# Three half-precision products in place of fp32 for kernel spectra and direct transforms in an S4 convolution and SwiGLU kernel

## The chip, the cores and the metric

The kernel runs on one core of a Trainium2 chip. The metric is device time in microseconds (us) of one execution; three executions before the change took 1172.26 to 1174.25 us, with a median of 1174.09 us. The engines are TensorE (PE, its weight loads PEld), VectorE (DVE), ScalarE (ACT), GpSimd (POOL) and SyncE (SP, which issues most DMAs). Each takes its instructions in the order of its own queue, and waits on semaphores for the others.

## The reference

Two layers, each an S4 convolution with a residual and a SwiGLU feed-forward network with a residual, on a sequence of L = 2048 rows with D = 512 channels; F = 1376, N = 128 states. Both layers use the same weights, so the convolution kernel K is formed once.

```python
def _A_ref(u, A_re, A_im, B_re, B_im, C_re, C_im, log_dt, Dskip):
    dt = jnp.exp(log_dt)[:, None]
    logdA = dt * (A_re + 1j * A_im)
    dB = dt * (B_re + 1j * B_im)
    P = jnp.exp(logdA[:, :, None] * l[None, None, :])
    K = jnp.einsum("dn,dnl,dn->dl", Cc, P, dB).real
    ...
    Yf = Uf * Kf[None, :, :, :]
    ...
    y = y + u * Dskip[None, None, :]

def _B_ref(x, w_gate, w_up, w_down):
    return (_silu(x @ w_gate) * (x @ w_up)) @ w_down

x = x + _A_ref(_layernorm(x), ...)
x = x + _B_ref(_layernorm(x), ...)
x = x + _A_ref(_layernorm(x), ...)
x = x + _B_ref(_layernorm(x), ...)
```

## The kernel before

**Stages.** The sequence is cut into four blocks of T = 512 rows. A block's transform is a product with constant factors of 128 by 128 (four residues q, real and imaginary part). Ahead of the blocks the kernel forms the convolution kernel's 2048 lags for 512 channels, in eight chunks of 64 channels, and transforms them. Then the eight pairs (layer, block) of SEQ follow, each an `ssm` (multiply by the spectra, inverse transform, residual) and an `ffn`.

**Order.** Everything up to the first `ffn` is traced inside `tc.manual_schedule` for ACT, DVE and PE: the order of each of these engines is the program's order, written by hand with generators, of which `take(it, n)` runs the next n steps. DMAs on SP are placed by a planner. A tile of a tag with n buffers waits until an earlier tile of that tag is done with. Tag "w" has three buffers of 2 KB per partition, "uu" three, and the PSUM tags "big" two and "sml" four.

**Start-up.** `stats` and `norm_early` normalise block 0 on DVE, `gen_w` forms the weights w0 (B, C and dt) on DVE, `gen_exp` and `gen_trig` run exponentials, sines and cosines on ACT. `direct` transforms block 0 straight from its rows with factors `ef` and `ek` (eight generators fw; the first step is the matmuls, L286, the second the eviction on ACT, L289). Block 1 is normalised (L964), written to `ndr`, and transformed by `second` one piece per pass and by two `early` pieces.

**The loop over chunks i = 0 to 6.** `lags` (L510, L511) forms chunk i's lags by small matmuls `pk`; ACT evicts them (`spread_in`, L516), PE rearranges them (`spread`, L526, L528, with the skip weights added by a matmul of one row), ACT evicts the result as `kt` (L1042), and `spectra` multiplies it with the factors (L547) for the four residues. ACT evicts each spectrum (L556, L558), and DVE (`wrap`, L584, L586) or POOL combines parts that go to `wdr`. Meanwhile DVE runs `gen_g` and `gen_e` for chunk i + 1 (L467 to L499 and L450 to L459) and `gen_turns` and `gen_reduce` for chunk i + 2 (L365 to L388). `gen_mags` (matmuls L438, exponentials L441) and `gen_trig` (L395 to L397) run for chunk i + 2. `norm_units` loads pieces of the FFN weights into tag "w", squares them on ACT (L316) and sums them on PE (L320). `sizes` sums the magnitudes of `kt` on ACT (L602); `product_scale` later makes from them a power of two, `sy`, by which products of blocks 1 and up are scaled ahead of half precision.

**The loop's order around `kt`.** `take(gg, 2)`, the last two steps of `gen_g`, ends with L499:

```python
            kp = spread(i, ks)
            if more:
                f = second(*sec[i])
                next(f)
            take(gg, 2)
            if more:
                tr = gen_trig(ts[i + 2])
                take(tr, 1)
            kt = kt2[:, 0]
            A.activation(kt, kp, AF.Copy)
            take(tr, 1)
```

**After the loop** the last chunk's lags and spectra are interleaved with `ssm(0, 0)`, whose inverse transform stays in fp32 (L781 with `ei`), and then the first `ffn` starts. From block 2 on, `forward` already uses three half-precision products, with the factors `eh` loaded then.

Of the kernel before, what the change touches and what calls it, by code (L numbers as in the profile page):

```python
# [41 lines left out]
HALF = 2  # L42
# [4 lines left out]
def dft_constants():  # L47
# [34 lines left out]
def kernel(ctx, tc, x, a_re, a_im, b_re, b_im, c_re, c_im, log_dt, d_skip,  # L82
                           w_gate, w_up, w_down, c_ef, c_ei, c_ek, c_am, c_eh, c_eih, out):
# [65 lines left out]
    hpi = sb.tile([P, 1], F32, name="hpi")  # L149
# [5 lines left out]
    ndr = dram.tile([2, 2, P, 2, HD], F32, name="ndr")  # L155
# [34 lines left out]
    nc.sync.dma_start(dsk, d_skip)  # L190

# [47 lines left out]
    def forward(n, h, eh):  # L239
# [13 lines left out]
        for i, q in enumerate(QORD):  # L253
            z = z2[:, 0 if eh else i % 2]
# [3 lines left out]
            if eh:  # L258
                hl = z2[:, 1].bitcast(F16).rearrange("p i (l d) -> p l i d", l=2)
                A.activation(hl[:, 0], z, AF.Copy, scale=256.0)  # L260
                stt(hl[:, 1], z, 256.0, hl[:, 0], OP.subtract)
            pf = psml([P, 2, HD], "pf")
            with tc.high_priority(offset=BOOST):
                for o in range(2):
                    if eh:
                        terms = [(eh[:, q, o + i, le], hl[:, lz, i]) for i in range(2) for le, lz in ((0, 0), (0, 1), (1, 0))]
                    else:
                        terms = [(ef[:, q, o + i], z[:, i]) for i in range(2)]
# [3 lines left out]
                A.activation(u, pf, AF.Copy, scale=2.0 ** -16 if eh else 1.0)  # L272
# [6 lines left out]

    def direct(b, h, q, n, space=psml):  # L280
# [8 lines left out]
        A.activation(u, pf, AF.Copy)  # L289
# [224 lines left out]
    def spread_in(pk):  # L514
        ks = tl([P, 4, 16, 16], "ks", "nn")
        A.activation(ks, pk.rearrange("p d (c a) -> p a c d", a=4), AF.Copy)  # L516
        return ks

    def spread(ch, ks):
# [3 lines left out]
        for grp in range(4):  # L523
            d0 = ch * DC + 16 * grp
            for ga in range(4):
                PE.matmul(kp[32 * ga:32 * ga + 32, grp], lhsT=ident[:, 32 * grp:32 * grp + 32], rhs=ks[:, ga],  # L526
                          start=True, stop=ga > 0, tile_position=(0, 32 * ga))
            PE.matmul(kp[0:32, grp, 0], lhsT=ident[0:1, 0:32], rhs=dsk[:, d0:d0 + 16], start=False, stop=True,  # L528
                      tile_position=(0, 0))
        return kp  # L530

    def spectra(ch, kt, k0, k1, qs=QORD, late=False):
# [4 lines left out]
        for q in qs:  # L537
# [6 lines left out]
            for i, c in [(i, c) for c in range(4) for i in range(2)] if k1 == 1 else \  # L544
                        [(i, c) for i in range(2) for c in range(4)]:
                e = ek[q // 2][:, q % 2, c - 1, i] if c else ef[:, q, i]
                PE.matmul(pw[:, i], lhsT=e, rhs=kt[:, :, c + 4 * k0:4 * k1:4, :].rearrange("p g k d -> p k g d"), start=c == 0, stop=c == 3)  # L547
                if k0 == 1 and (i, c) == (0, 3):
                    yield
# [140 lines left out]
    def inputs():  # L690

        for layer, b in SEQ:
# [17 lines left out]
            if (layer, b) == SEQ[HALF]:  # L710
                eh.append(tl([P, 4, 3, 2, P], "eh", "ef", F16))
# [213 lines left out]
    with tc.manual_schedule(engines={mybir.EngineType.Activation, mybir.EngineType.DVE, mybir.EngineType.PE}):  # L925
# [20 lines left out]
        for f in fw:  # L946
            next(f)
# [240 lines left out]
```

## Time and profile before

| | |
|---|---|
| median of three executions | 1174.09 us |
| span of the profiled execution | 1173.0 us |
| lag products of chunk 0 start | 58.7 us |
| lag products of chunk 7 end | 275.3 us |
| first FFN product starts | 320.5 us |

The profile comes from one execution. A line of a timeline has the start, the duration, the engine, the line of the program, the operation, out<-in with shapes, the count of merged instructions, and in brackets the idle time ahead of it with what ended it. In a line of groups the busy time and the mean duration stand behind the bar, then the idle time with its releaser. A matmul's duration contains its latency, so that neighbours overlap; their spacing is read from merged runs.

### The profile page before, as it was taken

The numbers are of one execution on the slowest core, as the hardware profiler recorded it, in microseconds if no ns is written. First come the engines' busy times: TensorE is split into PE (matmuls) and PEld (weight loads), VectorE is DVE, ScalarE is ACT, GpSimd is POOL, SyncE is SP. The second block draws the span as 40 slices with busy tenths as digits, with TensorE's granted clock in tenths as the row PEclk, the third lists the DMA queues.
The fourth block names the chain that finished last, engine by engine and source line by source line (L and its number), as shares of the span: only waits on it lengthen the run. The fifth ranks groups of instructions, "written<-read, shape, count | busy, mean of one in ns | idle before, by whom it ended". The sixth has DMA issues, their size and how long they took to land.

```text
span 1173.0 us, 25233 instructions
## 1 busy us (share of the span) xinstructions
PE 1103.5 (94%) x10276; PEld 861.6 (73%) x10276; DVE 1019.0 (87%) x1669; ACT 617.2 (53%) x1151; POOL 117.0 (10%) x170
## 2 busy tenths in 40 slices
PE   4899998989789989999999999999999999999998
PEld 3777777767675957686868687868777686876875
DVE  8999999997899999999998999999995999973211
ACT  6989898952382644537644533665434452333211
POOL 3110200013300010101000000211000000000000
PEclk9999999999999999999999999999999999999999
DMA  7454445576695237322253535342444144311000
GB/s 258 135 157 120 118 119 123 132 190 192 192 283 183 78 111 206 121 95 91 87 162 98 161 121 173 97 142 89 139 134 156 63 123 144 113 32 37 15 23 18
DMA packets 139174, 147.55 MB, mean 126 GB/s; under 512 B 78449, under 2 KB 87665, under 8 KB 139058
## 3 DMA queue, kind: packets, MB, share of 16 engines
q1 hardware_dynamic: 134194, 129.17, 36.4%
q0 software_dynamic: 4864, 16.78, 6.0%
q8 instruction: 80, 1.31, 0.5%
q14 instruction: 36, 0.29, 0.1%
HBM read 98.71 MB, written 28.31 MB: 108 GB/s over the span
## 4 chain that ended last, share of the span: by engine, by line
PE 40%; DVE 30%; ACT 13%; issue 9%; DMA 5%; POOL 2%; SPq 1%; DVEq 0%; ACTq 0%; POOLq 0%
PE pgu L886 6%; PE pgu L887 6%; PE pgu L888 6%; DVE yk L765 4%; DVE t L762 4%; PE pi L781 4%; PE pw L547 4%; PE py L900 3%; PE py L901 3%; PE py L902 3%; DVE z L226 2%; DVE yk L762 2%; PE pf L270 2%; DVE bt L226 2%; PE pk L510 2%
## 5 line engine op out<-in xcount | busy, mean ns | idle before, releaser
L886 PE MATMUL pgu<-mix,wsl 128*128 128x256 f16 x1280 | 350.5, 274 | 8.6 <-DVE sg L892 2.4
L887 PE MATMUL pgu<-mix,wsl 128*128 128x256 f16 x1280 | 350.6, 274 | 0.0
L888 PE MATMUL pgu<-mix,wsl 128*128 128x256 f16 x1280 | 350.5, 274 | 0.0
L887 PEld LDWEIGHTS <-wsl 128*128 128x128 f16 x1280 | 125.8, 98 | 24.7 <-issue 9.9
L888 PEld LDWEIGHTS <-wsl 128*128 128x128 f16 x1280 | 125.8, 98 | 15.1
L886 PEld LDWEIGHTS <-wsl 128*128 128x128 f16 x1280 | 125.8, 98 | 14.9
L900 PE MATMUL py<-wsl,hh 128*128 128x512 f16 (+1 forms) x352 | 133.6, 381 | 0.4 <-DVE sgr L862 0.4
L902 PE MATMUL py<-wsl,hl 128*128 128x512 f16 (+1 forms) x352 | 132.8, 381 | 0.0
L901 PE MATMUL py<-wsl,hh 128*128 128x512 f16 x320 | 121.5, 381 | 0.0
L762 DVE TENSOR_TENSOR t<-uu,w 128x1024 f32<-128x1024 f32 x96 | 117.5, 1224 | 0.5 <-DVE rs L222 0.3
L765 DVE TENSOR_TENSOR yk<-yk,t 128x1024 f32<-128x1024 f32 x96 | 117.5, 1224 | 0.2
L891 ACT ACTIVATE sg<-pgu,sc 128x512 f32<-128x512 f32 x80 | 54.6, 683 | 104.9 <-PE pgu L888 96.4
L892 DVE SCALAR_TENSOR_TENSOR sg<-pgu,sc,sg 128x512 f32<-128x512 f32 x80 | 60.0, 750 | 46.3 <-ACT sg L891 46.2
L781 PE MATMUL pi<-yl,mix 128*128 128x256 f16 x672 | 92.8, 273 | 6.4 <-ACT yl L770 5.5
L547 PE MATMUL pw<-kt,ek 128*128 128x256 f32 (+2 forms) x420 | 95.9, 365 | 0.0
L893 ACT ACTIVATE hh<-sg 128x512 f16<-128x512 f32 x80 | 50.0, 626 | 69.4 <-DVE sg L892 69.3
L547 PEld LDWEIGHTS pw<-kt,ek 128*128 128x128 f32 x420 | 76.3, 190 | 9.1
L270 PE MATMUL pf<-z,eh 128*128 128x256 f16 x576 | 75.0, 272 | 2.1 <-DVE z L226 1.7
L781 PEld LDWEIGHTS <-mix 128*128 128x128 f16 x672 | 65.3, 98 | 14.2 <-issue 1.1
L770 ACT ACTIVATE yl<-mix,sy 128x512 f16<-128x512 f32 x56 | 40.2, 718 | 59.1 <-DVE mix L767 58.8
L762 DVE TENSOR_TENSOR yk<-u,w0r 128x1024 f32<-128x1024 f32 x56 | 68.5, 1223 | 0.4 <-ACT u L272 0.4
L894 DVE TENSOR_TENSOR hl<-sg,hh 128x512 f16<-128x512 f32 x80 | 55.2, 691 | 13.5 <-ACT hh L893 13.5
(248 smaller groups left out, 2167.0 us busy)
## 6 DMA issues: line engine op xcount, KB each, us to landing
w<-wdr SPq DMA_DIRECT2D x96, 256.0 KB, 2.7
uu<-udr SPq DMA_DIRECT2D x96, 256.0 KB, 3.0
udr<-u POOLq DMA_DIRECT2D x32, 256.0 KB, 2.7
wdr<-wo SPq DMA_DIRECT2D x96, 64.0 KB, 2.6
udr<-u SPq DMA_DIRECT2D x16, 256.0 KB, 2.2
g<-tmp POOLq DMA_DIRECT2D x8, 512.0 KB, 4.6
g<-btl POOLq DMA_DIRECT2D x8, 512.0 KB, 5.9
n<-xdr SPq DMA_DIRECT2D x4, 1024.0 KB, 5.6
```

What stands on the lines that cost most here:

```text
L270: PE.matmul(pf[:, o], lhsT=e, rhs=m, start=k == 0, stop=k == len(terms) - 1)
L547: PE.matmul(pw[:, i], lhsT=e, rhs=kt[:, :, c + 4 * k0:4 * k1:4, :].rearrange("p g k d -> p k g d"), start=c == 0, stop=c == 3)
L762: V.tensor_tensor(t, uu.unsqueeze(1).to_broadcast([P, 2, 2, HD]), w.unsqueeze(2).to_broadcast([P, 2, 2, HD]), OP.mult)
L765: V.tensor_tensor(yk, yk, t, OP.add)
L781: PE.matmul(pi[:, o], lhsT=e, rhs=m, start=k == 0, stop=k == len(terms) - 1)
L886: PE.matmul(o, lhsT=wgu(wi, k, 0)[:, fs], rhs=nh[:, k], start=k == 0, stop=False)
L887: PE.matmul(o, lhsT=wgu(wi, k, 0)[:, fs], rhs=nlo[:, k], start=False, stop=False)
L888: PE.matmul(o, lhsT=wgu(wi, k, 1)[:, fs], rhs=nh[:, k], start=False, stop=k == 3)
L892: V.scalar_tensor_tensor(sg, pgu[:, 1], sc6[:, 4:5], sg, OP.mult, OP.mult)
L900: PE.matmul(py, lhsT=hh[:n, f, rc], rhs=wd(f, 0)[:n], start=f == 0, stop=False)
L901: PE.matmul(py, lhsT=hh[:n, f, rc], rhs=wd(f, 1)[:n], start=False, stop=False)
L902: PE.matmul(py, lhsT=hl[:n, f, rc], rhs=wd(f, 0)[:n], start=False, stop=f == FT - 1)
```

## The change

Spectra and direct transforms no longer multiply fp32 operands. Each operand is split into a half-precision value and its half-precision remainder, and a product becomes three: high by high, low by high, high by low. The factors come split from the host. The rows of block 0 and of block 1 and the lags are split on the chip: ACT copies (and so rounds) to half precision, DVE subtracts the copy. The lags are scaled by a power of two in `spread_in`; it comes from a bound on the lags, formed once in start-up by `bounds`, which also gives the scales of the products, so that `sizes` and `product_scale` go. The factor table `eh`, loaded late before, is loaded in place of `ef` at the start. The skip weights are added by two matmuls of one row in place of four.

```diff
-    ef = tl([P, 4, 3, P], "ef", "ef")
-    nc.sync.dma_start(ef, c_ef)
-    ek = [tl([P, 2, 3, 2, P], f"ek{i}", tag) for i, tag in enumerate(("hh", "hl"))]
+    eh = tl([P, 4, 3, 2, P], "eh", "ef", F16)
+    nc.sync.dma_start(eh, c_eh)
+    ek = [tl([P, 2, 3, 2, 2, P], f"ek{i}", tag, F16) for i, tag in enumerate(("hh", "hl"))]
...
+    def bounds():
+        grow, fall, mag = (tl([P, D], n, "w") for n in ("grow", "fall", "mag"))
...
+        A.activation(grow, rho, AF.Exp, scale=float(L - 1))
+        A.activation(fall, rho, AF.Exp, scale=256.0)
+        yield
+        A.activation(wa, w0, AF.Abs)
+        A.activation(ads[0:1, :D], dsk, AF.Abs)
+        A.activation(ads[0:1, D:2 * D], dsk, AF.Abs, scale=1.0 / 256)
+        yield
+        V.tensor_scalar(grow, grow, 1.0, 1e30, OP.max, OP.min)
+        V.tensor_scalar(fall, fall, 1.0, 7.0, OP.min, OP.mult)
+        V.tensor_tensor(wa[:, 0], wa[:, 0], wa[:, 1], OP.add)
+        V.tensor_tensor(sums[:, 0], wa[:, 0], grow, OP.mult)
+        V.scalar_tensor_tensor(sums[:, 1], fall, 1.0, sums[:, 0], OP.add, OP.mult)
+        yield
+        pb = pbig([P, 2, D], "pb")
...
+        yield
+        top = e0[:, :2]
+        V.tensor_reduce(top, pb, axis=AX.X, op=OP.max)
...
+        V.tensor_scalar(dsk, dsk, sy[0:1, 3:4], None, OP.mult)
+        yield
...
         for i in range(2):
             for c in range(4):
-                e = ek[q // 2][:, q % 2, c - 1, i] if c else ef[:, q, i]
-                PE.matmul(pf[:, i], lhsT=e, rhs=n[c], start=c == 0, stop=c == 3)
+                for le, ln in ((0, 0), (1, 0), (0, 1)):
+                    PE.matmul(pf[:, i], lhsT=factor(q, c, i, le), rhs=n[c][ln], start=c == le + ln == 0, stop=c == 3 and ln == 1)
...
-        A.activation(ks, pk.rearrange("p d (c a) -> p a c d", a=4), AF.Copy)
+        A.activation(ks, pk.rearrange("p d (c a) -> p a c d", a=4), AF.Copy, scale=sy[:, 3:4])
...
+    def halves(kt, kp):
+        A.activation(kt[:, 0], kp, AF.Copy)
+        yield
+        V.tensor_tensor(kt[:, 1], kp, kt[:, 0], OP.subtract)
+        yield
...
-            for i, c in [(i, c) for c in range(4) for i in range(2)] if k1 == 1 else \
-                        [(i, c) for i in range(2) for c in range(4)]:
...
+            for i in range(2):
+                terms = [(c, le, 0) for c in range(4) for le in range(2)] + [(c, 0, 1) for c in range(4)]
+                for c, le, lk in terms:
+                    PE.matmul(pw[:, i], lhsT=factor(q, c, i, le),
+                              rhs=kt[:, lk, :, c + 4 * k0:4 * k1:4, :].rearrange("p g k d -> p k g d"),
+                              start=c == le + lk == 0, stop=(c, lk) == (3, 1))
...
-    def sizes(ch, kt, junk):
-    def product_scale():
...
         take(ex, 11)
+        take(bnd, 1)
         norm_early(xe, ne, stats_x)
+        nhl = xe.bitcast(F16).rearrange("p c (l d) -> p l c d", l=2)
+        for c in range(0, 4, 2):
+            A.activation(nhl[:, 0, c:c + 2], ne[:, c:c + 2], AF.Copy)
+            V.tensor_tensor(nhl[:, 1, c:c + 2], ne[:, c:c + 2], nhl[:, 0, c:c + 2], OP.subtract)
         gen_w()
...
-        for f in fw:
+        for f in fw[:4]:
+            next(f)
+        take(bnd, 3)
+        for f in fw[4:]:
             next(f)
...
         take(fw[2], 1)
+        take(bnd, 1)
...
         take(fw[3], 1)
+        n1 = []
         for h in range(2):
             for cp in range(2):
-                nc.sync.dma_start(ndr[h, cp], x1[:, 2 * cp:2 * cp + 2, h * HD:(h + 1) * HD])
+                t = tl([P, 2, 2, HD], "n1", "w", F16)
+                xv = x1[:, 2 * cp:2 * cp + 2, h * HD:(h + 1) * HD]
+                A.activation(t[:, 0], xv, AF.Copy)
+                V.tensor_tensor(t[:, 1], xv, t[:, 0], OP.subtract)
+                nc.sync.dma_start(ndr[h, cp], t)
+                n1 += [(t[:, 0, c], t[:, 1, c]) for c in range(2)]
...
-        early = [direct(1, h, q, [x1[:, c, h * HD:(h + 1) * HD] for c in range(4)]) for h, q in sec[-2:]]
+        early = [direct(1, h, q, n1[4 * h:4 * h + 4]) for h, q in sec[-2:]]
...
-            A.activation(kt, kp, AF.Copy)
+            hv = halves(kt, kp)
+            take(hv, 2)
...
-                sizes(i, kt, ks)
...
-        A.activation(kts[1], kp, AF.Copy)
-        sizes(i, kts[1], ks)
+        hv = halves(kts[1], kp)
+        take(hv, 2)
...
-        pscale = product_scale()
-        take(pscale, 1)
```

More of the change, by code (lines that the diff above doesn't have):

```diff
@@ L154 @@
     xdr = dram.tile([NB, 4, P, D], F32, name="xdr")
-    ndr = dram.tile([2, 2, P, 2, HD], F32, name="ndr")
+    ndr = dram.tile([2, 2, P, 2, 2, HD], F16, name="ndr")
     e0, er_, ep = (sb.tile([P, 4], F32, name=f"e{i}") for i in range(3))
@@ L190 @@
     nc.sync.dma_start(dsk, d_skip)
+    def bounds():
+        grow, fall, mag = (tl([P, D], n, "w") for n in ("grow", "fall", "mag"))
+        ads = tmp[1].rearrange("p s d -> p (s d)").bitcast(BF16)
+        sums = mag.bitcast(BF16).rearrange("p (i d) -> p i d", i=2)
+        wa = btl[:, :4 * HD].rearrange("p (i d) -> p i d", i=2)
+        A.activation(grow, rho, AF.Exp, scale=float(L - 1))
[13 more added lines that the diff above has]
+        for i in range(2):
+            PE.matmul(pb[:, i], lhsT=onesb, rhs=sums[:, i], start=True, stop=False)
+            PE.matmul(pb[:, i], lhsT=onesb[0:1], rhs=ads[0:1, i * D:(i + 1) * D], start=False, stop=True)
+        yield
+        top = e0[:, :2]
+        V.tensor_reduce(top, pb, axis=AX.X, op=OP.max)
+        V.tensor_scalar(top, top, 1.02, None, OP.mult)
+        e, b = top.bitcast(I32), sy.bitcast(I32)
+        V.tensor_scalar(e, e, 23, None, OP.logical_shift_right)
+        V.tensor_scalar(e, e, 40, 240, OP.max, OP.min)
+        V.tensor_scalar(b[:, 3:4], e[:, 0:1], -1, 268, OP.mult, OP.add)
+        V.tensor_scalar(b[:, 2:3], e[:, 0:1], 1, -22, OP.mult, OP.add)
+        V.tensor_scalar(b[:, 1:2], e[:, 1:2], 1, -5, OP.mult, OP.add)
+        V.scalar_tensor_tensor(b[:, 0:1], e[:, 0:1], 97, e[:, 1:2], OP.add, OP.subtract)
+        V.tensor_scalar(b[:, :4], b[:, :4], 23, None, OP.logical_shift_left)
+        V.tensor_scalar(sy[:, 4:6], sy[:, 1:3], -1.0, None, OP.mult)
+        V.tensor_scalar(dsk, dsk, sy[0:1, 3:4], None, OP.mult)
+        yield
     def stats(src, rows, scale, tag="stats", between=None):
@@ L278, in norm_early, with factor @@
             V.tensor_scalar(n[:, c], xt[:, c], rs[:, c:c + 1], nb[:, c:c + 1], OP.mult, OP.add)
+    def factor(q, c, i, part):
+        return ek[q // 2][:, q % 2, c - 1, i, part] if c else eh[:, q, i, part]
     def direct(b, h, q, n, space=psml):
@@ L543, in spectra @@
                 pw = psml([P, 2, nk, 4, 16], "pw")
-            for i, c in [(i, c) for c in range(4) for i in range(2)] if k1 == 1 else \
-                        [(i, c) for i in range(2) for c in range(4)]:
-                e = ek[q // 2][:, q % 2, c - 1, i] if c else ef[:, q, i]
-                PE.matmul(pw[:, i], lhsT=e, rhs=kt[:, :, c + 4 * k0:4 * k1:4, :].rearrange("p g k d -> p k g d"), start=c == 0, stop=c == 3)
-                if k0 == 1 and (i, c) == (0, 3):
+            for i in range(2):
+                terms = [(c, le, 0) for c in range(4) for le in range(2)] + [(c, 0, 1) for c in range(4)]
[3 more added lines that the diff above has]
+                              start=c == le + lk == 0, stop=(c, lk) == (3, 1))
+                if k0 == 1 and i == 0:
                     yield
@@ L722, in ssm @@
         half = SEQ.index((layer, b)) >= INV
+        back, less = (sy[:, 1:2], sy[:, 4:5]) if half else (sy[:, 2:3], sy[:, 5:6])
         if (layer, b) == SEQ[INV]:
@@ L733, in combine @@
                     bb[q] = tl([P, 2, HD], "bb", "bb")
[L734 removed]
+                    A.activation(bb[q], pi, AF.Copy, scale=back)
                     return
@@ L737, in combine @@
                 bb[q] = tl([P, 2, HD], "dd", "dd")
-                if half:
-                    stt(bb[q], pi, sy[:, 2:3], s, OP.add)
-                    stt(s, pi, sy[:, 1:2], s, OP.add)
-                else:
-                    V.tensor_tensor(bb[q], s, pi, OP.subtract)
-                    V.tensor_tensor(s, s, pi, OP.add)
+                stt(bb[q], pi, less, s, OP.add)
+                stt(s, pi, back, s, OP.add)
             late = []
@@ L933, in turns @@
             take(gen_turns(0, ts[0]), 2)
-        stats_x = stats(xe, 4, 1.0, between=turns)
+        stats_x = stats(xe, 4, 256.0, between=turns)
+        bnd = bounds()
         take(gen_reduce(ts[0]), 9)
@@ L1128 @@
         take(rest, 1)
-        take(pscale, 1)
         take(first, 2)
```

87 lines of the change are left out of this document (32 added, 55 removed).

## The prediction

> **What bounds the kernel now.** I read the page's first part, then busy time in four stretches: start-up, the loop over seven chunks of lags, the first block, the rest.
>
> ```profile
> span 1173.0 us, 25233 instructions
> PE 1103.5 (94%) x10276; PEld 861.6 (73%) x10276; DVE 1019.0 (87%) x1669; ACT 617.2 (53%) x1151; POOL 117.0 (10%) x170
> ...
> 59.00:250.00 191.00, 176.59 (x2597) 140.97 (x2594) 184.44 (x291) 164.22 (x287) 21.66 (x32) 0.97 0.54 132
> 250.00:320.00 70.00, 61.42 (x609) 51.35 (x608) 57.77 (x99) 22.27 (x35) 20.61 (x29) 0.99 0.65 188
> 320.00:1173.00 853.00, 826.18 (x6912) 637.25 (x6911) 725.35 (x1187) 381.01 (x724) 59.37 (x73) 0.99 0.38 114
> ```
>
> The columns are PE, PEld, DVE, ACT, POOL. The change works ahead of 320 us alone. There, in the loop, DVE is busy 184.4 of 191 us, PE 176.6 and ACT 164.2: three engines near their limit, each in program order. What counts is who waits for whom. So I read the timeline of one pass (chunk 2), engine by engine:
>
> ```profile
> 173.82 1.21 DVE L499 SCALAR_TENSOR_TENSOR btl<-g,xi 128x1024 f32<-128x1024 f32 x1
> 174.96 2.21 DVE L456 SCALAR_TENSOR_TENSOR im<-im,mu 128x1984 f32<-128x1984 f32 x1
> 177.09 0.35 DVE L584 TENSOR_TENSOR wo<-s 128x192 f32<-128x192 f32 x1
> 177.36 1.18 DVE L459 TENSOR_TENSOR re<-re,mu 128x992 f32<-128x992 f32 x1
> 178.46 0.34 DVE L586 TENSOR_TENSOR wo<-s 128x192 f32<-128x192 f32 x1
> 178.73 1.18 DVE L459 TENSOR_TENSOR re<-re,mu 128x992 f32<-128x992 f32 x1
> ...
> 164.19 1.00 ACT L1042 ACTIVATE kt<-kp 128x1024 f32<-128x1024 f32 x1
> 174.41 1.02 ACT L441 ACTIVATE re<-pm 128x1024 f32<-128x1024 f32 x1
> 175.33 1.23 ACT L316 ACTIVATE sq<-st 128x344 bf16<-128x344 f32 x3
> 176.47 0.58 ACT L556 ACTIVATE s<-pw 128x512 f32<-128x512 f32 x1
> ...
> 166.46 0.59 PE L547 MATMUL pw<-kt,ef 128*128 128x256 f32 x2
> 169.91 0.60 PE L438 MATMUL pm<-kt,btl 112*128 112x512 bf16 x2
> 178.13 0.60 PE L438 MATMUL pm<-kt,btl 112*128 112x512 bf16 x2
> ...
> L1042 ACT ACTIVATE kt<-kp x7: 1002/1004/1024, 72.6 to 257.0; 128x1024 f32<-128x1024 f32 x7
> ```
>
> ACT has kt at 165.2 and PE starts the spectra (L547) at 166.5, long before DVE finishes L499 at 175.0. The evicted first spectrum (L556) is ready at 177.05, just as DVE comes to L584. A pass takes (257.0 - 72.6)/6 = 30.7 us. By the end of the second L459 the five passes after chunk 0 average 30.6; 24.9 of it (again their mean) is DVE from that point to the end of L499, nearly without a gap.
>
> **The change, part by part.** *Matmuls.* An fp32 product is two records, a half-precision one is one; spacing comes from runs in the chain:
>
> ```profile
> 258.06 7.17 PE pw L547 x32
> 371.14 1.20 PE pi L781 x11
> 319.23 1.23 DVE L832 TENSOR_TENSOR mix<-pt,mix 128x1024 f16<-128x1024 f32 x1 [3.77 <-ACT mix L830]
> ```
>
> 7.17/32 = 0.224, at best 0.215, so one fp32 product is 0.43 us; 1.20/11 = 0.109, three make 0.327. Some 360 products of 256 columns save 0.10 each, 37 us of PE. A spectrum or transform (8 products) falls from 3.45 to 2.6. The trace has no half-precision moving operand in runs of 16 elements. Bounds: 0.109 and the fp32 spacing 0.215; I take 0.109, since strided pw and contiguous fp32 matmuls have the same spacing.
>
> *The subtraction in the loop.* `halves` puts kt's low part on DVE. By program order it stands behind take(gg, 2), so behind L499. Like L832 (PSUM in, f16 out) it takes 1.2 us. PE's first spectrum must stop after 8 of 24 products until it is done; pm, two more spectra and the next lag products queue behind it, and behind pm stand ACT's L441, the squares, L556, and so DVE's L584. From the end of L499: subtraction 1.2, 16 products 1.75, pm 0.6, semaphores 0.2, L441 0.92, squares 1.13, L556 0.58, then L584, L459, L586, L459 2.85: 9.25 us in place of 4.9 (174.96 to 179.91). A pass becomes 24.9 + 9.25 = 34.2, **+3.6 for each of five passes, +18**. PE's own queue gives nearly the same (the next lag products 0.7 later). Bounds for a pass: +0.2 (only 1.2 us of DVE, less a mean idle of 1.0) and, with 0.215 spacing, +8.
>
> *Start-up.* The rows are in order of time, by engine:
>
> ```profile
> 18.01 1.92 DVE L278 TENSOR_SCALAR xne<-xne,rs 128x512 f32<-128x512 f32 x4
> 19.83 1.22 DVE L183 TENSOR_TENSOR bw<-bw,dt 128x1024 f32<-128x1024 f32 x1
> 24.94 0.64 DVE L467 TENSOR_TENSOR xr<-xr,mzp 128x384 f32<-128x384 f32 x1
> 31.60 0.19 DVE L474 TENSOR_TENSOR g<-g,wx 128x64 f32<-128x64 f32 x1
> 35.76 0.56 DVE L385 TENSOR_TENSOR xi<-xi,xr 128x384 f32<-128x384 f32 x1 [1.75 <-ACT xr L376]
> 50.85 2.35 DVE L453 TENSOR_TENSOR re<-re 128x1024 f32<-128x1024 f32 x2
> ...
> 27.02 1.93 ACT L412 ACTIVATE re<-rho 128x64 f32<-128x64 f32 x12
> 34.74 0.58 ACT L289 ACTIVATE u<-pf 128x512 f32<-128x512 f32 x1
> 45.02 0.57 ACT L289 ACTIVATE u<-pf 128x512 f32<-128x512 f32 x1
> 57.64 1.00 ACT L441 ACTIVATE mu<-pm 128x992 f32<-128x992 f32 x1
> 60.37 1.69 ACT L316 ACTIVATE sq<-st 128x512 bf16<-128x512 f32 x3
> ...
> 58.73 0.48 PE L510 MATMUL pk<-re,g 128*32 128x64 f32 x5 [0.42 <-issue]
> ...
> L893 ACT ACTIVATE hh<-sg 128x512 f16<-128x512 f32 x80 | 50.0, 626 | 69.4 <-DVE sg L892 69.3
> L894 DVE TENSOR_TENSOR hl<-sg,hh 128x512 f16<-128x512 f32 x80 | 55.2, 691 | 13.5 <-ACT hh L893 13.5
> ...
> ndr<-x SPq DMA_DIRECT2D x4, 256.0 KB, 2.5
> st<-in_B_w_down_dram SPq DMA_DIRECT2D x10, 256.0 KB, 3.5
> ```
>
> A 128x512 split costs ACT about 0.55 and DVE 0.6 (L893, L894 less overlap), a 128x1024 one 1.0 and 1.2.
> (a) ACT's copies of the normalised block stand behind eleven of L412's exponentials, which end at 28.8, and two new ones (to 29.8). DVE, done with L278 at 19.9, waits for the first copy until 30.8 and subtracts until 33.2. gen_w (L183 on) starts 13.4 late and ends at 38.3.
> (b) ACT's Abs of w0 waits for that: 38.3, 2.0 of Abs, 40.4. The exponentials left over (28.8 to 34.74) follow: the first eviction comes at 46.3.
> (c) DVE sums the bound (five operations, 3.0) to 41.4, does what ran from 24.94 to 31.60 by 48.0, and the maximum with ten small operations (3.4) by 51.4. The 1.75 wait at L385 goes; L453's end moves from 53.1 to 71.2.
> (d) ACT waits for L385 (54.3), reaches the eviction of 45.02 at 59.8, and makes three of the four copies of the second block. All come from tag "w", three buffers; the fourth needs the first one's, free when its DMA has landed: subtraction at 71.8, issue and landing (2.5) 74.5, copy 75.1. ACT's work from 45.5 to 58.7 follows, so chunk 0's lag products start at 88.3 in place of 58.73: **+29.5**. Without that buffer, DVE alone gives 71.2 + 2.4 + 4.4 + 1.1 = 79, +20. With the added DVE work only (2.4 + 3.0 + 3.4 + 2.4), +11.
>
> *Chunk 0's pass.* Three weight tiles that had been loaded early (squares, L316 at 60.37, ahead of the lags' eviction) share "w" too. The second and third wait for the second block's last tiles, read by a transform behind the lag products (6.4 + 2.6), then issue and load (0.5 and 3.5): squares end at +14 after the start of the lag products, where eviction came at 6.5. That costs DVE 7; with the late subtraction less this pass's old idle, **+10** (bound below +2).
>
> *Tail, 250 to 320 us.* Chunk 6 stands even (PE's saving against the wait for L499). Then:
>
> ```profile
> 285.63 0.69 DVE L742 TENSOR_TENSOR dd<-bb,pi 128x512 f32<-128x512 f32 x1 [2.05 <-PE pi L781]
> ...
> L516 ACT ACTIVATE ks<-pk 128x1024 f32<-128x1024 f32 x8 | 8.2, 1025 | 28.3 <-PE pk L511 28.3
> ```
>
> From 285.6 DVE runs without a gap to the first FFN's statistics, so PE's saving there ends no wait; the nine small operations of product_scale save 1.5, and the dropped load of the second factor table some DMA time: **-2** (0 to -8). The sums of magnitudes leave ACT, which waits 28.3 us ahead of the lags' evictions anyway: nothing. Scaling inside evictions and fewer one-row matmuls: nothing, no instruction more.
>
> Sum: 29.5 + 10 + 18 - 2 = +55.5. On 1173.0 that is 1228.5; the median lies 1.1 higher: **1229.6**.
>
> **Rivals.**
> (1) *Buffers do not bind* (ACT's fourth copy and the weight tiles find room): 20 + 3.5 + 18 - 2 = +39.5, 1213. For it: allocation can't be seen in a trace. Against: squares at 60.37 show tiles taken long ahead.
> (2) *Only added work counts*, the orders being such that no wait forms: 11 + 2 + 2 - 2 = +13, 1187. Against: ACT and DVE are in order in every row above.
> (3) *Short runs slow the products* to 0.215: five passes at +8, chunk 0 and the tail 5 more each: 1263.
> (4) *Faster: the subtraction follows kt at once.* Place: DVE before L493 rather than after L499. Then the loop keeps its time, if the start-up's work also falls into gaps; the tail gives -6 to -8 with PE's saving and the load on the path: 1167. It decides if the subtraction ends by 168. Against: DVE's queue has no gap there.
> (5) *PE is the bound everywhere*: -37, 1137. By busy time PE leads with 94%.
>
> [...]
>
> **How the numbers follow.** Forecast 0.52; rival 1 0.18; rival 2 0.13; rival 3 0.06; rival 4 0.07; rival 5 0.02; nothing measurable 0.02. Range: forecast, rivals 1 and 2 with their bounds, 1185 to 1245, 0.83. Faster 0.09, same 0.02, slower 0.89; 0.2% is about what can be told from no change.
>
> **What would show it.** DVE idle from 20 to 31 us behind an ACT copy; ACT idle ahead of the Abs and the fourth copy; lag products first at about 88; in each pass PE idle inside the first spectrum, until the subtraction behind L499, and DVE idle at the wrap's first row for some 3 us; kt's period 34; from the first FFN on, the same length as before. Wrong: a period of 31 or less (the subtraction hidden), or a start below 80 (the buffers).

## The result, and the profile after

The changed kernel takes **1248.3 us** (median of four runs, 1244.7 to 1253.4) against 1173.8 us before: a ratio of 1.063 with a 95% interval of 1.060 to 1.066. The prediction said 1229.6 us, with a range of 1185 to 1245: the direction is right, the size is not, and the time lies just outside the range. The profiled execution took 1244.7 us with a span of 1242.9, so the spans differ by 69.9 us where the working had +55.5. It is the fastest of the four executions, so the landmarks below account for 69.9 of the 74.6 us between the medians.

The first fence is the page's first part for the changed kernel, the second its busy time by stretch (columns: PE, PEld, DVE, ACT, POOL, granted clock, share of DMA, GB/s). The stretches meet at the first lag products, kt of chunk 5, and the first product of the feed-forward part.

```profile
span 1242.9 us, 26002 instructions
PE 1075.0 (86%) x10655; PEld 830.2 (67%) x10655; DVE 1035.0 (83%) x1690; ACT 618.4 (50%) x1146; POOL 114.7 (9%) x170
```
```profile
0.00:87.00 87.00, 37.19 (x236) 27.60 (x236) 62.29 (x119) 55.85 (x118) 12.84 (x36) 0.88 0.41 131
87.00:285.00 198.00, 141.19 (x2475) 106.98 (x2474) 167.24 (x260) 143.32 (x246) 20.58 (x30) 0.87 0.45 111
285.00:393.00 108.00, 72.00 (x1035) 58.46 (x1035) 81.58 (x129) 38.52 (x62) 18.80 (x31) 0.87 0.57 156
393.00:1242.00 849.00, 824.63 (x6912) 637.12 (x6911) 723.88 (x1186) 380.74 (x724) 62.47 (x73) 0.99 0.38 114
```

TensorE's busy time fell by 28.5 us (1103.5 to 1075.0), so the products did become cheaper, and the span still grew. Ahead of 393 us the granted clock is 0.87 to 0.88; in the two middle stretches of before that the prediction shows it was 0.97 and 0.99. Behind 393 us hardly anything has changed (849.9 us to the end in place of 852.5).

The next table holds the landmarks that all later readings use, in us from the start of each profiled execution: the first lag product (pk) of chunk 0, the start of ScalarE's copy into kt for chunks 0, 5 and 7, the first feed-forward product, the span. "Pass" is (kt 5 - kt 0)/5.

| kernel | median | pk 0 | kt 0 | kt 5 | kt 7 | feed-forward | span | pass |
|---|---|---|---|---|---|---|---|---|
| before | 1173.8 | 58.7 | 72.6 | 225.9 | 280.2 | 320.5 | 1173.0 | 30.6 |
| after | 1248.3 | 87.7 | 105.5 | 284.6 | 345.1 | 393.0 | 1242.9 | 35.8 |
| e1_early_sub | 1240.8 | 87.1 | 106.4 | 271.3 | 341.8 | 390.9 | 1241.5 | 33.0 |
| e2_fill | 1237.2 | 87.8 | 104.5 | 276.0 | 336.4 | 385.3 | 1235.3 | 34.3 |
| e3_block1 | 1239.3 | 80.4 | 95.3 | 274.3 | 338.0 | 385.3 | 1237.0 | 35.8 |
| e4_tail | 1240.8 | 87.5 | 104.8 | 283.9 | 346.8 | 389.1 | 1239.7 | 35.8 |
| e5_start | 1238.2 | 80.5 | 98.1 | 276.5 | 337.6 | 385.4 | 1235.2 | 35.7 |
| e6_early2 | 1225.1 | 87.6 | 104.0 | 268.8 | 324.9 | 374.1 | 1224.6 | 33.0 |
| e7_warm | 1233.7 | 92.4 | 105.3 | 275.0 | 332.0 | 379.9 | 1230.5 | 33.9 |
| e8_all | 1201.2 | 75.0 | 89.0 | 254.1 | 310.6 | 350.9 | 1198.9 | 33.0 |
| e9_pe_lo | 1198.9 | 74.9 | 88.9 | 251.1 | 305.4 | 346.5 | 1197.2 | 32.4 |
| e10_hi_only | 1194.8 | 71.2 | 86.4 | 249.4 | 300.6 | 342.2 | 1192.6 | 32.6 |
| e11_hi_no_sub | 1193.1 | 71.7 | 87.1 | 241.2 | 299.5 | 340.3 | 1191.4 | 30.8 |
| e12_no_bound | 1200.7 | 73.5 | 87.2 | 252.4 | 309.9 | 350.2 | 1199.2 | 33.0 |

From before to after: +28.9 up to pk 0, +3.9 to kt 0, +25.9 in five passes, +6.2 to kt 7, +7.6 to the feed-forward part, -2.6 behind it. The kernel before was run beside each group of experiments, at medians of 1173.1 to 1174.5. The changed kernel's four runs spread by 0.7%, so a gain of an experiment over it is read from the landmarks first.

**The start** came as forecast. The fence has rows of the timeline of after: start, duration, instruction, and in brackets the idle time ahead of it and what ended that.

```profile
31.20 2.36 DVE L965 TENSOR_TENSOR xne<-xne 128x1024 f16<-128x1024 f32 x2 [10.78 <-ACT xne L964]
...
38.45 1.06 ACT L197 ACTIVATE btl<-w 128x1024 f32<-128x1024 f32 x1 [6.34 <-DVE w L183]
...
46.52 0.60 ACT L323 ACTIVATE u<-pf 128x512 f32<-128x512 f32 x1
...
74.00 0.63 ACT L1002 ACTIVATE n<-x 128x512 f16<-128x512 f32 x1 [12.51 <-DMA ndr<-n]
...
87.66 0.40 PE L544 MATMUL pk<-re,g 128*32 128x64 f32 x3 [0.34 <-issue]
```

VectorE stands 10.8 us behind ScalarE's copy, ScalarE 6.3 us behind w0 and 12.5 us in front of the fourth copy, which the store of the first one released.

**One pass** (chunk 2 here) shows the wait and something that the forecast did not have.

```profile
175.91 1.00 ACT L571 ACTIVATE kt<-kp 128x1024 f16<-128x1024 f32 x1
...
185.50 1.22 DVE L533 SCALAR_TENSOR_TENSOR btl<-g,xi 128x1024 f32<-128x1024 f32 x1
186.63 1.22 DVE L573 TENSOR_TENSOR kt<-kp,kt 128x1024 f16<-128x1024 f32 x1
187.76 2.21 DVE L490 SCALAR_TENSOR_TENSOR im<-im,mu 128x1984 f32<-128x1984 f32 x1
...
187.90 0.37 PE L592 MATMUL pw<-kt,eh 128*128 128x256 f16 x1 [9.90 <-DVE kt L573]
...
192.08 1.04 ACT L475 ACTIVATE re<-pm 128x1024 f32<-128x1024 f32 x1 [5.88 <-PE pm L472]
...
194.76 0.36 DVE L631 TENSOR_TENSOR wo<-s 128x192 f32<-128x192 f32 x1 [4.79 <-ACT s L603]
```
```profile
176.97:178.00 1.03, 1.03 (x8) 0.77 (x8) 1.03 (x4) 0.95 (x1) 0.89 (x3) 1.00 0.77 231
187.90:191.05 3.15, 3.15 (x15) 2.17 (x15) 2.08 (x1) 0.00 (x0) 0.00 (x0) 0.50 0.99 190
191.70:197.00 5.30, 5.30 (x47) 4.45 (x46) 2.24 (x4) 4.51 (x9) 0.00 (x0) 1.00 0.25 68
```

The subtraction stands behind L533, TensorE stops for 9.9 us after 8 products, and VectorE comes to the wrap's first row 4.8 us too early: all as forecast, the last one longer (forecast: some 3 us). New is the granted clock (the third number from the end) in the second fence, which is the view by stretch: 1.00 ahead of the wait, **0.50 in the 3.15 us behind it**, 1.00 again after that. The products that VectorE then waits for run at a spacing of 0.21 us in place of 0.109.

**The tail** went against the forecast:

```profile
346.16 1.23 DVE L573 TENSOR_TENSOR kt<-kp,kt 128x1024 f16<-128x1024 f32 x1 [14.39 <-ACT kt L571]
...
349.12 3.41 PE L801 MATMUL pi<-yf,mix 128*128 128x256 f32 x8 [4.05 <-DVE yf L786]
```

VectorE stands 14.4 us in front of the last chunk's subtraction, since the first block's multiplications (L782) stand behind it in its order.

### The profile page after: what moved, and what is told of

The parts are those of the page before. It is cut to its first block, busy times and chain, and to the rows that moved or that the text cites. A ratio compares the mean times of both kernels' runs of the same rounds, so it can differ in the third digit from the quotient of the medians.

```text
span 1242.9 us, 26002 instructions
## 1 busy us (share of the span) xinstructions
PE 1075.0 (86%) x10655; PEld 830.2 (67%) x10655; DVE 1035.0 (83%) x1690; ACT 618.4 (50%) x1146; POOL 114.7 (9%) x170
## 4 chain that ended last, share of the span: by engine, by line
PE 29%; DVE 28%; issue 9%; DMA 3%; ACT 3%; POOL 1%; SPq 0%; DVEq 0%; POOLq 0%; ACTq 0%
DVE t L782 5%; PE pgu L906 5%; PE pgu L907 5%; PE pgu L908 5%; DVE yk L785 4%; PE pi L801 3%; DVE z L261 3%; PE py L920 3%; PE py L921 3%; PE py L922 3%; DVE yk L782 2%; PE pf L301 2%; DVE bt L261 1%; DVE sg L912 1%; DMA mix<-nn 1%
## 5 line engine op out<-in xcount | busy, mean ns | idle before, releaser
L908 PE MATMUL pgu<-mix,wsl 128*128 128x256 f16 x1280 | 350.2, 274 | 0.7 <-DVE wsl L684 0.7
L920 PE MATMUL py<-wsl,hh 128*128 128x512 f16 x352 | 133.2, 379 | 0.0
L921 PE MATMUL py<-wsl,hh 128*128 128x512 f16 x320 | 121.0, 379 | 0.0
L782 DVE TENSOR_TENSOR t<-uu,w 128x1024 f32<-128x1024 f32 x96 | 117.4, 1223 | 0.5 <-DMA uu<-udr 0.3
L592 PEld LDWEIGHTS <-ek 128*128 128x128 f16 x630 | 61.9, 104 | 69.1 <-issue 59.0
L592 PE MATMUL pw<-kt,eh 128*128 128x256 f16 (+2 forms) x210 | 47.4, 283 | 64.6 <-DVE kt L573 57.7
L592 PE MATMUL pw<-kt,ek 128*128 128x256 f16 (+2 forms) x630 | 90.7, 282 | 0.0
L782 DVE TENSOR_TENSOR yk<-u,w0r 128x1024 f32<-128x1024 f32 x56 | 68.4, 1221 | 0.0
L914 DVE TENSOR_TENSOR hl<-sg,hh 128x512 f16<-128x512 f32 x80 | 55.2, 690 | 14.5 <-ACT hh L913 14.4
```

The lines of the kernel that those rows point to most:

```text
L592: PE.matmul(pw[:, i], lhsT=factor(q, c, i, le), rhs=kt[:, lk, :, c + 4 * k0:4 * k1:4, :].rearrange("p g k d -> p k g d"), start=c == le + ...
L782: V.tensor_tensor(t, uu.unsqueeze(1).to_broadcast([P, 2, 2, HD]), w.unsqueeze(2).to_broadcast([P, 2, 2, HD]), OP.mult)
L908: PE.matmul(o, lhsT=wgu(wi, k, 1)[:, fs], rhs=nh[:, k], start=False, stop=k == 3)
L920: PE.matmul(py, lhsT=hh[:n, f, rc], rhs=wd(f, 0)[:n], start=f == 0, stop=False)
L921: PE.matmul(py, lhsT=hh[:n, f, rc], rhs=wd(f, 1)[:n], start=False, stop=False)
```

## The experiments

The theory after the result: no single engine's work pays for the change, but waits made by order, and each can be taken away alone. The rivals were that the products themselves are slow, that the added work counts alone, or that the waits cover one another.

**e1_early_sub.** The subtraction ahead of the last doublings of g, as in rival 4 of the prediction:

```
             take(sp, 1)
-            take(gg, 1)
-            wrap()
-            take(gg, 1)
-            wrap()
             kp = spread(i, ks)
...
-            take(gg, 2)
...
             take(hv, 2)
+            take(gg, 1)
+            wrap()
+            take(gg, 1)
+            wrap()
+            take(gg, 2)
```

> Edit: in the chunk loop the remainder's subtraction (L573) stands ahead of the last two doublings of g (from L520 on) in VectorE's order, instead of behind L533; nothing is added or left out. Theory A (the wait is what a pass pays): kt's copy ends about 0.9 us before VectorE reaches that place, so the subtraction waits for nothing, TensorE's 8 to 10 us idle inside the first spectrum goes, the wrap's first row follows L490 at once, and a pass falls from 35.2 us to between 30.7 (the pass before) and 32 (that plus the subtraction's 1.2). Six passes: 1218 to 1228 us. Rival B (only the added work counts): no work is taken away, so the time stays within 3 us of 1247. Rival C (the short half-precision products run slowly in themselves, spacing 0.21 us): the spacing stays at 0.21 without the idle time, and a pass stays over 34 us: 1240 to 1247.

A miss: 1240.8 us, a time in rival C's range. Yet the wait goes (from chunk 1 on, TensorE's idle time inside the first spectrum is 0.23 us) and the spacing there is 0.109, so rival C falls. In chunk 0 the spacing is still 0.21: there TensorE stood 2.29 us ahead of the spectrum, and the clock was 0.58 on the mean of the next 3.1 us. But a pass falls to 33.0, not to 32 or less, and the last one gives back most of what was won: kt 5 is 13.3 us earlier than in the changed kernel, the feed-forward part 2.1. Rows of e1's timeline around chunk 7's lag products:

```profile
311.46 8.37 POOL L610 COPY w0r<-s 128x128 f32<-128x128 f32 x1 [28.19 <-ACT s L603]
...
321.55 0.88 POOL L529 DMA_DIRECT2D g<-tmp  x1
...
329.45 0.48 PE L544 MATMUL pk<-re,g 128*32 128x64 f32 x5 [15.56 <-DMA g<-btl]
```

GpSimd's order is not written out by hand; in e1 a copy of the spectra came to stand ahead of the two DMAs that add into g, and the lag products waited 15.6 us for these.

**e6_early2.** The same edit in the passes of chunks 0 to 5 alone:

```
-            take(gg, 1)
-            wrap()
-            take(gg, 1)
-            wrap()
+            if not more:
+                for g in (gg, None, gg, None):
+                    take(g, 1) if g else wrap()
...
-            take(gg, 2)
+            else:
+                take(gg, 2)
...
             take(hv, 2)
+            if more:
+                for g in (gg, None, gg, None, gg, gg):
+                    take(g, 1) if g else wrap()
```

> Edit: as in e1_early_sub the subtraction stands ahead of L520, but only in the passes that make spectra behind it (chunks 0 to 5); chunk 6 keeps the old order. Theory A (in e1 a pass fell to 33.0 us and the gain was given back in the last pass, where GpSimd's copy of 8.4 us at L610 came to stand ahead of the DMA that adds into g, so that the lag products of chunk 7 waited 15.6 us for it): chunk 7's lag products start 30 to 31 us after chunk 6's in place of 38.8, and the time is 1230 to 1235 us. Rival B (the last pass gives it back whatever GpSimd's order is): 1239 to 1243. The pass itself: 33 us in both, since the chain through g's DMA (6.6 us from the last product on VectorE to its landing), the lag products and kt is what it now waits for.

1225.1 us, some 5 us under theory A's range: chunk 7's lag products start 28.1 us after chunk 6's (315.2 and 287.1) in place of 38.8. The pass is 33.0, as expected from e1. Its rows in e6 show what ends last now:

```profile
113.27 1.22 DVE L533 SCALAR_TENSOR_TENSOR btl<-g,xi 128x1024 f32<-128x1024 f32 x1
...
118.84 1.19 DVE L493 TENSOR_TENSOR re<-re,mu 128x992 f32<-128x992 f32 x1
...
121.55 0.49 PE L544 MATMUL pk<-re,g 128*32 128x64 f32 x5 [4.02 <-DMA g<-btl]
```

TensorE is through with the spectra and stands 4.0 us for the DMA that adds L533's product into g. In other passes the profile names an eviction there, but the distance is what stays: 7.1 us here from L533's end (114.49) to the first lag product, 6.6 to 7.5 in all six passes, and 5.8 to 7.4 in the same place of the kernel before. So the faster products bought idle time on TensorE.

**e2_fill.** The order of the changed kernel, with TensorE kept at work during its wait in chunks 0 to 5 (`zero` is a tile of zeros):

```
                 for c, le, lk in terms:
+                    if late and i == 0 and q == qs[0] and (c, lk) == (0, 1):
+                        for _ in range(64):
+                            PE.matmul(pw[:, 0], lhsT=zero, rhs=kt[:, 0, :, 0:16:4, :].rearrange("p g k d -> p k g d"),
+                                      start=False, stop=False)
```

> Edit: the order stays that of the changed kernel; behind the first 8 products of each chunk's first spectrum stand 64 products with a weight tile of zeros, which add nothing to the sum, so that TensorE works through most of its wait for the subtraction (64 x 0.109 = 7.0 us of the 8 to 10 us idle). Theory A (the granted clock falls because TensorE stood idle): the 16 products behind the wait run at a spacing of 0.11 us in place of 0.21, which takes 16 x 0.1 = 1.6 us off the path of each pass, 8 to 12 us in all: 1235 to 1240 us. Rival B (the spacing of 0.21 has another cause, such as the just written remainder being read, or a clock held down by the work done): the spacing stays and the time stays within 3 us of 1247, or is longer.

1237.2 us, as theory A had it, though 384 products were added. The 64 did not always reach to the end of the wait, which makes a second experiment of it. The first fence is from the timeline of e2, the second from its view by stretch:

```profile
148.16 0.27 PE L598 MATMUL pw<-kt,eh 128*128 128x256 f16 x1 [2.13 <-DVE kt L575]
...
183.47 0.27 PE L598 MATMUL pw<-kt,eh 128*128 128x256 f16 x1 [3.10 <-DVE kt L575]
```
```profile
148.20:151.00 2.80, 2.80 (x25) 2.31 (x25) 2.04 (x1) 0.47 (x1) 0.00 (x0) 1.00 1.01 189
183.47:186.59 3.12, 3.12 (x17) 2.20 (x17) 2.08 (x1) 0.00 (x0) 0.00 (x0) 0.55 0.99 190
```

Where 2.13 us of idle time were left, 25 products took 2.8 us at a clock of 1.00; where 3.10 were left, 17 took 3.1 us at 0.55. That pass lasted 36.7 us, the two behind it, with 1.9 and 1.8 us left, 34.0. So the idle time makes the spacing, not the short runs of 16 elements (the products and the shapes of their operands are the same in both).

**e7_warm.** e6_early2 with 40 products by zeros (`warm`) ahead of the lag products of chunks 0 to 6, through the 4 us wait for g:

```
         pk = pbig([P, 16, 64], "pk")
+        for _ in range(warm):
+            PE.matmul(pk[:, :4], lhsT=zero, rhs=eh[:, 0, :2].rearrange("p i l r -> p (i l r)")[:, :256], start=True, stop=True)
```

> Edit: e6_early2 with 40 products by a weight tile of zeros ahead of each chunk's lag products, into the tile that these overwrite, so that TensorE works through its 4 us wait for g's DMA. Theory A (the clock falls when TensorE stands idle for some us, and the lag products behind the wait last 6.5 to 7.3 us in place of 5.4 to 6.1 for that reason): they last 5.3 to 5.9 us, and with six such passes the time is 4 to 7 us under e6_early2's. Rival B (they last longer because of g's late arrival, chunk by chunk, or the added products themselves delay them): they last 6.5 us or more, or start later, and the time is e6_early2's or above.

Slower than e6 by 8.5 us: rival B, for a reason that its sentence holds only in part. One chunk's lag products in e6, then in e7, by stretch:

```profile
220.19:227.77 7.58, 6.07 (x257) 5.87 (x258) 7.58 (x18) 1.25 (x3) 0.00 (x0) 0.76 0.57 160
```
```profile
226.22:233.21 6.99, 4.74 (x258) 4.42 (x258) 6.09 (x12) 0.00 (x0) 0.21 (x1) 1.00 0.38 107
```

The clock is back at 1.00 and TensorE's busy time falls from 6.07 to 4.74 us, but the stretch from first to last product hardly gets shorter (6.5 us in place of 6.8 on the mean of chunks 1 to 6), and it starts later (7.6 to 8.9 us after the last doubling of g in place of 6.6 to 7.5), since the added products wait for a PSUM buffer until an eviction of ScalarE's (0.8 us idle ahead of the first of them in four of these six chunks, put down to L477) and then take 4.5 us or more. Here the faster clock gained less than the products that made it cost: a pass is 1 us longer.

**e3_block1, e5_start, e4_tail** each take one wait of the start or the tail away. e3: the remainders of block 1 ahead of L527, and the last early transform ahead of the lag products.

```
-        for g in (gg, ge, gg, rd, gg, rd, rd, gg, rd, rd, gg, rd, gg, rd, gg, rd, gg, ge, gg, ge, ge):
+        for g in (gg, ge, gg, rd, gg, rd, rd, gg, rd, rd, gg, rd, gg, rd, gg, rd):
...
+        for g in (gg, ge, gg, ge, ge):
+            take(g, 1)
         sec = [(h, q) for h in range(2) for q in QORD]
...
+            if i == 0:
+                take(early[1], 1)
             pk = lags(ts[i], gs[i])
-            if i == 0:
-                take(early[1], 1)
```

> Edit: the remainders of block 1 (L1003) stand ahead of L527 in VectorE's order instead of behind L487, so that their stores leave about 8 us earlier and free the w buffer for the fourth copy; and the last early transform of block 1, which holds two w buffers, stands ahead of chunk 0's lag products on TensorE instead of behind them. Theory A (a w buffer held by a store is what ScalarE's fourth copy waits for): the fourth copy runs at about 66.5 in place of 74.0, the lag products of chunk 0 start at 79 to 81 in place of 87.6, and the squares of chunk 0 no longer wait 4 us for a load: 1233 to 1240 us. Rival B (VectorE's own work sets the start and the wait lies beside it): the copy runs earlier, but the lag products start at 86 or later: 1243 to 1248.

e5: copies of block 0 ahead of the exponentials, gen_w ahead of the subtractions, the bound's sums later.

```
-        take(ex, 11)
-        take(bnd, 1)
         norm_early(xe, ne, stats_x)
+        gen_w()
...
-        gen_w()
+        take(ex, 11)
+        take(bnd, 1)
```

> Edit: at the start, ScalarE's copies of block 0 stand ahead of L446's eleven exponentials, the five operations of gen_w ahead of the subtractions on VectorE, and the absolute values and sums of bounds() behind VectorE's next four operations. Theory A (steps a and b of the prediction: order alone makes VectorE stand 10.8 us and ScalarE 6.3 us): the subtractions run at 27 to 30 us in place of 31.2 to 33.5, gen_w ends at 25 to 26, the first eviction is at 39 to 41 in place of 46.5, and the lag products of chunk 0 start at 77 to 80 in place of 87.6: 1237 to 1241 us. Rival B (the fourth copy's w buffer alone sets the start): the start stays at 85 or later, 1244 to 1248.

e4: the last chunk's subtraction behind the first half's four multiplications.

```
         hv = halves(kts[1], kp)
-        take(hv, 2)
+        take(hv, 1)
...
         take(first, 2)
+        take(hv, 1)
```

> Edit: the last chunk's subtraction stands behind the first block's first four multiplications by the spectra in VectorE's order, instead of ahead of three of them. Theory A (VectorE stood 14.4 us in front of that subtraction with work behind it that was ready): the multiplications fill that time, and the first feed-forward stage starts 6 to 8 us earlier: 1239 to 1242 us. Rival B (from there on TensorE at a low clock sets the end, with its inverse products of 3.4 and 4.0 us): the multiplications come earlier and the stage starts within 2 us of before: 1245 to 1248.

All three by theory A: 1239.3, 1238.2 and 1240.8 us. Rows of e3, then of e5:

```profile
64.47 0.63 ACT L1002 ACTIVATE n<-x 128x512 f16<-128x512 f32 x1 [3.76 <-DMA ndr<-n]
...
80.36 0.37 PE L544 MATMUL pk<-re,g 128*32 128x64 f32 x8
```
```profile
26.74 2.36 DVE L964 TENSOR_TENSOR xne<-xne 128x1024 f16<-128x1024 f32 x2 [1.61 <-ACT xne L963]
...
39.69 0.58 ACT L323 ACTIVATE u<-pf 128x512 f32<-128x512 f32 x1
...
66.86 0.63 ACT L1002 ACTIVATE n<-x 128x512 f16<-128x512 f32 x1 [12.47 <-DMA ndr<-n]
```

In e3 the fourth copy waits 3.8 us in place of 12.5 and the lag products start 7.3 us earlier; one of chunk 0's squares still waits 3.2 us for its load. In e5 VectorE's 10.8 us shrink to 1.6, and the start moves by 7.1 us (to 80.5, where 77 to 80 was expected) although the fourth copy's wait stays: the two waits stand one behind the other. In e4 kt 7 to the feed-forward part takes 42.3 us against 47.9 after and 40.3 before; -5.6 us, a little less than the 6 to 8 expected.

**e8_all.** e6, e3, e4 and e5 together, the same work in another order.

> Edit: e6_early2, e3_block1, e4_tail and e5_start together; the same work as in the changed kernel, in another order. Theory A (the waits found are separate terms that add up: loop 13, block 1's copy 8, start order 8, tail 6 us): 1207 to 1216 us, which is still above the kernel before, since VectorE's and ScalarE's added work (about 10 us ahead of the first lag products, 1.2 us in each pass) stays on the path. Rival B (the waits cover one another): 1220 us or more. Rival C (the faster products gain once the order is right): below 1172.

1201.2 us, ratio 1.024 (1.023 to 1.026), under theory A's 1207 to 1216, whose terms were too small. The four gains over 1248.3 (23.2, 9.0, 7.5 and 10.1) add to 49.8, and 47.1 came: separate terms. It is still 28 us above the kernel before, run beside it. The spans of the two profiles differ by 25.9: +16.2 up to pk 0, +11.9 in five passes, +2.2 from kt 5 to kt 7, and -4.5 behind the start of the feed-forward part; kt 7 to that start takes 40.2, as before.

**e10_hi_only and e11_hi_no_sub** ask what of that is TensorE's, and what the subtraction's. Both leave work out, as their expectations say.

```
-                terms = [(c, le, 0) for c in range(4) for le in range(2)] + [(c, 0, 1) for c in range(4)]
+                terms = [(c, 0, 0) for c in range(4)]
...
-                for le, ln in ((0, 0), (1, 0), (0, 1)):
-                    PE.matmul(pf[:, i], lhsT=factor(q, c, i, le), rhs=n[c][ln], start=c == le + ln == 0, stop=c == 3 and ln == 1)
+                PE.matmul(pf[:, i], lhsT=factor(q, c, i, 0), rhs=n[c][0], start=c == 0, stop=c == 3)
```

and in e11 alone

```
-        V.tensor_tensor(kt[:, 1], kp, kt[:, 0], OP.subtract)
```

> Edit: e8_all with one product of three in the spectra and the direct transforms, that of the two first halves; the two products with a remainder are left out (two thirds of TensorE's work there), the remainders are still made. Theory A (TensorE's products are off the path once the order is mended, so making them faster gains nothing): 1196 to 1202 us against e8_all's 1201. Rival B (TensorE's work at its present speed still sets the pass): 64 products of 0.109 us less are 7 us in each of seven passes: 1150 to 1165 us.

> Edit: e10_hi_only, and the remainder of kt isn't made either (those of the normalised blocks are). Theory A (the 1.2 us on VectorE is on the path of each pass, and of TensorE's work nothing is): 7 to 10 us under e10_hi_only, at 1188 to 1194 us, still above the kernel before by what the start costs (pk of chunk 0 at 75 in place of 58.7). Rival B (the pass is set by g's DMA and the lag products alone, and the subtraction lies beside them): within 2 us of e10_hi_only.

With two products of three left out, 6.4 us go; by landmarks 2.6 are gone by kt 0 and 2.2 in the five passes. Slightly more than theory A allowed, far from rival B: a pass goes from 33.0 to 32.6. With the subtraction gone as well, a pass is 30.8, the kernel before's 30.6. In time e11 shows only 1.7 us of that, which is what rival B had; the passes speak for theory A, and what they won went at the place where e1 lost its gain: chunk 7's lag products waited 8.4 us for g's DMA, ahead of which a copy of 3.8 us stood on GpSimd.

**e9_pe_lo.** e8_all with the remainder made off VectorE.

```
-        V.tensor_tensor(kt[:, 1], kp, kt[:, 0], OP.subtract)
+        for j in range(0, 4, 2):
+            PE.matmul(kp[:, j:j + 2], lhsT=minus, rhs=kt[:, 0, j:j + 2], start=False, stop=True, skip_group_check=True)
+        A.activation(kt[:, 1], kp, AF.Copy)
```

> Edit: e8_all with the remainder of kt made without VectorE: two products by a negative identity in half precision subtract the first half from kp where it lies, and ScalarE copies the rest as the second half. Theory A (VectorE's 1.2 us for the subtraction stands on the path of each pass, behind kt and ahead of the doublings of g): a pass falls from 32.5 to about 31.3 us, 7 to 9 us in all: 1192 to 1195 us. Rival B (ScalarE's second copy of 1.0 us, ahead of the sines that VectorE takes up next, costs as much as the subtraction did): 1198 to 1204 us.

1198.9 us, 2.3 under e8, in rival B's range. A pass falls by 0.6 us of the 1.8 that e11 showed. That ScalarE's second copy takes the rest is likely, but no run took it apart.

**e12_no_bound.** e8_all with constants for the scale factors:

```
-        A.activation(grow, rho, AF.Exp, scale=float(L - 1))
...
+        for k, f in ((0, -22), (1, -16), (2, -25), (3, 17)):
+            G.memset(sy[:, k:k + 1], 2.0 ** f)
```

> Edit: e8_all without the forming of the bound: the exponentials, absolute values, sums, products and small operations of bounds() are left out, and the scale factors are written as constants. Theory A (what the start still costs in e8_all, lag products of chunk 0 at 75 us in place of 58.7, is work that stands on VectorE and ScalarE: 6.4 us of the bound on VectorE with 3 us of waiting for its product, and the rest the remainders of the two blocks): chunk 0's lag products start at 66 to 69 us, the rest of the kernel keeps its length, and the time is 1192 to 1196 us. Rival B (another wait takes its place, such as the fourth copy's, and the start doesn't move by more than 2 us): 1198 to 1202 us.

A miss for theory A; rival B had it: the start moved by 1.5 us, the time by 0.5. Rows of GpSimd and ScalarE in e12, then the same GpSimd operation in e8:

```profile
36.03 7.05 POOL L213 TENSOR_SCALAR rs<-mv 128x4 f32<-128x4 f32 x1 [10.13 <-DVE mv L212]
43.16 5.63 POOL L214 TENSOR_TENSOR rs<-rs,fixed 128x4 f32<-128x4 f32 x1
...
49.41 2.93 ACT L969 ACTIVATE x<-x,rs 128x512 f32<-128x512 f32 x4 [4.66 <-POOL rs L216]
```
```profile
38.36 0.20 POOL L239 TENSOR_SCALAR rs<-mv 128x4 f32<-128x4 f32 x1 [12.84 <-DVE mv L238]
```

Two operations on 128x4 elements took 12.7 us, and ScalarE stood behind them. In e8 VectorE was waiting for the bound's product just then (some 3 us; 2.64 in e5, whose start has the same order), and the same operation took 0.20. So the price of the bound itself stays open: without it another wait stood in its place.

## Why the direction was right and the size was not

- **Products at 0.109 us.** Right where TensorE is kept busy (0.11 in e6's chunks 0 to 5 and e1's chunks 1 to 6). Behind the waits of after (6.8 to 9.9 us) they ran at 0.21, behind e2's 3.10 us at 0.18. Rival 3 had that spacing with another cause, the short runs, which e2 refutes (and its terms add to 1261.6, not 1263).
- **Start-up, +29.5.** Measured +28.9. Steps (a), (b) and (d) are the three waits in the rows of after, each within 0.7 us of its forecast time; e5 took away nearly all of the first and the whole second, e3 most of the third. Rival 1, that buffers do not bind, fell with the wait at L1002.
- **Chunk 0's pass, +10.** Measured +8.0 by the end of the second L493 (36.96 later than before, less 28.93). The wait for the weight tiles was over-sized, though: the last square ends 10.4 us after the start of the lag products, not 14, and the lags' eviction, and kt with it, comes 3.9 us later, where the working had 7; the rest of the pass costs 4.1, not some 3. That the sum came near is partly luck.
- **Five passes, +3.6 each.** The mechanism was right and the term too small: +5.1 by the same landmark, 7.5 us more in all than the +18. The step that fell short is "16 products 1.75": the 16 behind the wait last 3.0 to 3.4 us, because the clock had dropped to 0.50. By e2 and e6, of the 5.2 us by kt about 1.5 are the clock, 1.4 the rest of the late order, and 2.3 remain with the subtraction in its best place, of which it makes 1.8 itself (e11).
- **Tail, -2.** This step failed, and it is the larger part: from the end of pass 5 to the feed-forward part it was +10.1, then -2.6, in place of -2. "Chunk 6 stands even" was wrong: TensorE's late spectra hold up chunk 7's lag products, and kt 6 to kt 7 grew from 23.2 to 28.5. "From 285.6 DVE runs without a gap" was wrong too: it was read from the kernel before, and the subtraction, which the changed code puts ahead of three of those multiplications, makes a gap of 14.4 us there. e4 took 5.6 of the 7.6 us back by order alone. The prediction had worked out the same wait in the loop and did not ask for it at the place where the code takes the second pair of halves.
- **Together:** -0.6 - 2.0 + 7.5 + 9.5 = +14.4 us, the difference between 55.5 and 69.9.
- **Rival 4, the subtraction at once.** e1 and e6 tried it. It takes 1.2 us of VectorE in front of the doublings of g, and the pass is 33.0, not 30.6: VectorE, g's DMA, the lag products, kt form a ring in which TensorE's spectra have hardly a part (0.4 us a pass by e10). That alone keeps 1167 out of reach, and the start costs 16 us more on top.
- **Rival 5** fell for the same reason: e10 left out two thirds of these products and gained 6 us.

The missing term is the granted clock behind an idle gap on TensorE. The runs show it low behind short gaps too and without a sharp bound: 0.50 behind 9.9 us (after, chunk 2), 0.55 behind 3.10 and 1.00 behind 2.13 (both e2), and behind 2.29 us once 0.58 (e1, chunk 0) and once 1.00 (e8, chunk 0).

Open is how the 16 us that the start still costs in e8 divide between the bound, the remainders of the two blocks and the waits between them; e12 did not tell. It wasn't tried whether GpSimd's statistics done elsewhere would let the start move. No version came below the kernel before.

## What to carry to other kernels

A cheaper product gains only where the product is what ends last: follow the ring from a pass to the next, and ask whether the engine to be relieved is in it. A split into halves adds an operation to the engines beside TensorE, and where that operation stands in a hand-written order decides more than its 1.2 us: search for every place at which it is issued, and ask at each one what ready work is queued behind it. A wait can be paid twice: behind the waits that stopped TensorE for 6.8 to 9.9 us in after and for 3.10 us in e2 the clock was 0.50 and 0.55, and products that were waited for ran at 0.21 and 0.18 us in place of 0.109. So read the clock behind a wait before a spacing goes into a sum.

## What the chip showed that was not expected

- TensorE's granted clock: in each of the seven passes of after with an idle gap (6.8 to 9.9 us) the first 2.5 us behind it ran at 0.50, and 2.6 to 5.6 us after the gap's end the clock was back at 1.00. Behind 3.10 us it was 0.55, behind four others of e2's six filled waits, with gaps of at most 2.13 us, it was 1.00, and behind 2.29 us it went either way (0.58 in e1, 1.00 in e8): the length of the gap alone does not settle it.
- Small operations on GpSimd took very different times. In e12 one on 128x4 elements took 7.05 us and in e1 one on 128x128 took 8.37, with no gap above 0.1 us in VectorE's rows beside them. Against that stand 0.20 us in e8 for the same operation as in e12, where VectorE was waiting, and 0.29 us in e6 and in after for the same as in e1 (in after at 332.53, with VectorE idle from 331.8 to 346.2). That VectorE is at work does not settle it alone: in the kernel before, the 128x4 operation took 0.21 us at 31.77, and VectorE's rows have no gap from 28.4 to 33.9. No run took VectorE's work away, so the cause was not shown.
